# Own terms, output rows and score transposes of an RWKV-6 chunk kernel: other engines, another PSUM bank

## The chip, the cores and the metric

The kernel runs on one core of a Trainium2 chip. The metric is the device time of one execution in microseconds (us); the median of three runs of the kernel before is 248.56 us (248.35 to 248.85).

## The reference

Two blocks follow each other. The first is a recurrence over 768 positions for 4 batches x 8 heads with 48 features each; its output, written as rows of 384, is the input of a mixture-of-depths block, which picks the 128 best-scored rows of each batch, runs them through a feed-forward net and adds the gated result.

```
for t in range(S):
    cur = einsum('bhd,bhe->bhde', u * k_t, v_t)
    y[t] = einsum('bhd,bhde->bhe', r_t, state + cur)
    state = w_t * state + einsum('bhd,bhe->bhde', k_t, v_t)

scores = x @ w_gate                    # x: y as (batch, 768, 384)
top = the 128 largest of each batch
out[top] = x[top] + sigmoid(scores[top]) * (relu(x[top] @ w1) @ w2)
```

The term with `u` can be taken out of the recurrence: it adds to each row, head by head, the number sum over d of r x u x k (the *own* term), times v.

## The kernel before, in words

The sequence is cut into chunks of L = 128 positions, 6 to a batch, 24 in all (N = 24). For a chunk, the decays w are transposed (`decays_t`, L217, tile ps_w) and scanned from both sides on VectorE (`scans`, L221: right_buf, then left). r and k are transposed (`scaled`, L254, tile ps_t) and multiplied by the scans to R and K. `scores` (L274) multiplies K and R to ps_s; `masked` (L284) masks them to sc, in two VectorE instructions. `back` (L290) transposes K back and ScalarE copies it to kt. `outputs_t` (L297) multiplies sc with v and adds the product with the old state into ps_yt; ScalarE copies that to yt. `carry_products` (L350) makes the chunk's part of the state, ps_kv; `carry` (L362) adds it to the old state on VectorE (mid) and multiplies by the decays on POOL (state). A chunk that is the last of its batch has neither.

The own term: `own_products` (L260) makes r x k x u on POOL (tile rk, 128 x 8 heads x 48), `own_values` (L266) sums over the 48 to own (128 x 8) on VectorE and multiplies v by it on POOL (vo). `rows_out` (L321) transposes yt to ps_y, adds vo on VectorE into the rows x, and stores them by a DMA from the SP queue. `row_products` (L331, POOL) and `row_sums` (L335, ScalarE) make the score of each row.

The ranks need every score compared with every other. `compared_t` (L382) transposes a chunk's scores into a 128x128 tile ps_e and copies it on ScalarE to the tile every; `compared` (L397) counts on VectorE, first against the earlier chunks (L404), then against the chunk itself, read straight from ps_e (L408). After a batch's last chunk `mixture` (L413), a generator that `mix` runs a step at a time, makes ranks, picks, gathers the rows and computes the gate (with an exp on ScalarE). `forward` (L495) is the feed-forward net, cut in pieces that `fed` places between the other work of TensorE, in turns 10 and after.

The order is written by hand. `turn(i)` (L568) puts out the steps of several chunks: scores, mask, output and state of chunk i, K and R of i + 1, the decays of i + 2, the rows of i - 1, the comparisons of i - 2. Each engine works its own queue in that order. "Turn 3" in this text begins with the score products (ps_s) of chunk 3.

PSUM is split in pools with one tile buffer for each of their bufs. psW has one buffer, tag "w", used by ps_w and by ps_e. psK has one, tag "kv", used by ps_kv. psY has one, used by ps_yt and ps_y. psT has two, used by all ps_t. psS holds ps_s, psM the feed-forward net. Who takes a buffer waits until all readers of its last content are done.

Of the kernel before, what the change touches and what calls it, by code (L numbers as in the profile page):

```python
# [10 lines left out]
FP32 = mybir.dt.float32  # L11
# [3 lines left out]
AF = mybir.ActivationFunctionType  # L15
ALU = mybir.AluOpType
AX = mybir.AxisListType

L = 128
DP = 64  # L20
# [18 lines left out]
def kernel(  # L39
# [39 lines left out]
    nc = tc.nc  # L79
    PSUM = bass.MemoryType.PSUM  # L80

    B, H, S, D = r.shape
# [17 lines left out]
    psW = ctx.enter_context(tc.tile_pool(name="psW", bufs=1, space=PSUM))  # L100
# [3 lines left out]
    psK = ctx.enter_context(tc.tile_pool(name="psK", bufs=1, space=PSUM))  # L104
# [3 lines left out]
    N = len(chunks)  # L108
# [19 lines left out]
    def loads(n):  # L128

        load(v_bufs, v, n - 2)  # L130
        load(k_bufs, k, n - 1)
        load(r_bufs, r, n - 1)
        load(w_bufs, w, n)
# [22 lines left out]
    def load_weights(n):  # L156
        while n > 0 and weights:
            to, src = weights.pop(0)
            nc.sync.dma_start(out=to, in_=src)
            n -= 1  # L160
# [50 lines left out]
    def transposed(pool, tag, src):  # L211
        ps = pool.tile([L, HP, L], FP32, tag=tag, name=f"ps_{tag}")
        for j in range(HP):
            nc.tensor.transpose(ps[:, j, :], src(j), ident)  # L214
        return ps
# [48 lines left out]
        nc.gpsimd.tensor_mul(rk, rk, u_bc)  # L264

    def own_values(t):  # L266
        o = lev.tile([L, H], FP32, tag="own", name="own")
        nc.vector.tensor_reduce(out=o, in_=t.pop("rk"), axis=AX.X, op=ALU.add)  # L268
        t["vo"] = lev.tile([L, H, D], FP32, tag="vo", name="vo", bufs=3)
        nc.gpsimd.tensor_mul(  # L270
            t["vo"], v_bufs[t["n"] % VBUF][:, :, 0:D], o.to_broadcast([L, H, D])
        )
# [45 lines left out]
        t["yt"] = lev.tile([L, HP, L], FP32, tag="yt", name="yt")  # L318
        nc.scalar.copy(out=t["yt"], in_=ps)  # L319

    def rows_out(t):  # L321
        b, ci = chunks[t["n"]]
        ps = transposed(psY, "y", lambda j: t["yt"][:, j, :])
        x = t["x"] = lev.tile([L, C], FP32, tag="x", name="x", bufs=3)
        nc.vector.tensor_add(  # L325
            x.rearrange("p (h d) -> p h d", d=D),
            ps.rearrange("p j (q d) -> p (j q) d", d=DP)[:, :, 0:D], t.pop("vo"),
        )
        nc.sync.dma_start(out=views[b][b, ci * L:(ci + 1) * L, :], in_=x)

    def row_products(t):  # L331
# [10 lines left out]
    def row_scores_soon(t, x):  # L342
        b, ci = chunks[t["n"]]
        scr = lev.tile([L, C], FP32, tag="scr", name="scr")
        nc.vector.tensor_tensor_reduce(
            out=scr, in0=x, in1=wg_bc, scale=1.0, scalar=0.0, op0=ALU.mult, op1=ALU.add,
            accum_out=score[:, b, ci:ci + 1],
        )
# [33 lines left out]
    def compared_t(t):  # L382

        b, ci = chunks[t["n"]]
        if ci == 0:
            against[b] = (
                mod.tile([L, S - L], FP32, name="every", bufs=2),
                mod.tile([L, NCH, S], BF16, name="ahead", bufs=2),
                mod.tile([L, NCH, 2], FP32, name="lost", bufs=2),
            )  # L390
            nc.vector.memset(against[b][2][:, 0, 0:1], 0.0)
        t["e"] = ps = psW.tile([L, L], FP32, tag="w", name="ps_e")
        nc.tensor.transpose(ps, score[:, b, ci:ci + 1].to_broadcast([L, L]), ident)
        if ci < NCH - 1:
            nc.scalar.copy(out=against[b][0][:, ci * L:(ci + 1) * L], in_=ps)
# [137 lines left out]
    def step(f, n, *more):  # L533
        if 0 <= n < N:
            f(work.setdefault(n, dict(n=n)), *more)

    def mix(n=1):

        while n > 0 and mixing:
            try:  # L540
                next(mixing[0])
                n -= 1
            except StopIteration:
                mixing.pop(0)
# [14 lines left out]
    def fed_in_turn(n):  # L559

        if (feed or picked) and (feed or picked)[0][0] == B - 2:
            n = min(n, 1) if n < PIECES - PIECES // 2 else 0
        fed(n)
# [4 lines left out]
    def turn(i):  # L568
        step(own_products, i + 1)
        step(scores, i)  # L570
        step(masked, i)
        step(carry, i - 1, work.get(i))
        step(scaled, i + 1, "K", k_bufs, "right")
        step(back, i)
        step(rows_out, i - 1)
        if i == N:
            row_scores_soon(work[N - 1], work[N - 1]["x"])
        else:
            step(row_products, i - 1)
        step(compared_t, i - 2)  # L580
        step(compared, i - 2)
        mix()
        fed_in_turn(PIECES // 2)
        step(scaled, i + 1, "R", r_bufs, "left")
        step(decays_t, i + 2)
        step(outputs_t, i)
        step(carry_products, i)
        fed_in_turn(PIECES - PIECES // 2)
        step(scans, i + 2)
        step(range_check, i + 2)  # L590
        step(own_values, i + 1)
        if i < N:
            step(row_sums, i - 1)
        if 0 <= i - 2 < N and chunks[i - 2][1] == NCH - 1:
            mixing.append(mixture(chunks[i - 2][0]))
        mix()
        if i > -2:
            loads(i + 5)
        if i > 1:
            load_weights(1 if NCH > 2 else 100)  # L600

    with tc.manual_schedule():
        for i in range(-2, N + 1):
            turn(i)

        step(compared_t, N - 1)
        step(compared, N - 1)
        fed(NFC // 2)
        mixing.append(mixture(B - 1))
        mix(2)  # L610
        fed(NFC // 2)
        mix(2)
        fed(2 * NFC)
        mix(1000)
        fed(1000)


    def general(gen):
        u_t = gen.tile([D, H], FP32, name="u_t")
        nc.sync.dma_start(out=u_t, in_=u.rearrange("h d -> d h"))  # L620
        for b in range(B):
# [27 lines left out]
            for c in range(NCH):  # L649
                x = lev.tile([L, C], FP32, tag="x", name="x", bufs=3)  # L650
                nc.sync.dma_start(out=x, in_=out[b, c * L:(c + 1) * L, :])
                t = dict(n=b * NCH + c)
                row_scores_soon(t, x)
                compared_t(t)
                compared(t)
# [6 lines left out]
    ps = psM.tile([L, C], FP32, tag="m", name="ps_w")  # L662
# [3 lines left out]
        out=wide, in0=ps[0:1, 0:1], scalar1=0.0, scalar2=None, op0=ALU.is_gt  # L666
# [30 lines left out]
```

## Time and profile before

| | |
|---|---|
| median of 3 runs | 248.56 us |
| the profiled execution, its own time | 250.67 us |
| its span, first to last instruction | 248.9 us |
| TensorE busy | 209.1 us, 84% |
| VectorE busy | 193.7 us, 78% |
| ScalarE busy | 89.3 us, 36% |
| POOL busy | 107.3 us, 43% |

The profile is one execution, with the start and length of each instruction. PE is TensorE, PEld its weight loads, DVE VectorE, ACT ScalarE, POOL GpSimd, SP the engine that issues DMAs. A row of a timeline gives start, duration, engine, line, operation, the tile written and those read; what stands in square brackets is idle time of that engine just before, and who ended it. A row of the groups gives the count, the busy time in us, the mean of one in ns, and idle time before. A row of waits gives who waited for whom: total us, times, longest. Shares of busy time are means over the span; which wait ends last in a turn is read from its timeline.

### The profile page before, as it was taken

To read this page: it belongs to the slowest core of one execution; us is meant where nothing else is said; L and a number is where in the kernel's file an instruction comes from. 1 tells how busy PE (TensorE), PEld (TensorE's weight loads), DVE (VectorE), ACT (ScalarE), POOL (GpSimd) and SP (SyncE) were. 2 spreads that over 40 slices of the span, in tenths; PEclk is the share of its full clock that TensorE was granted. 3 is DMA by queue.
4 is the path that set the end of the run, shared out by engine and by line. 5 is a ranking of instruction groups with operands and counts; after the bars stand their busy time and mean duration, and the time that the engine had idled before them with its cause. 6 is when DMAs were issued, how large, how long until landed. Compare 5 with 4: busy or idle time off the path is not lost.

```text
span 248.9 us, 5967 instructions
## 1 busy us (share of the span) xinstructions
PE 209.1 (84%) x2290; PEld 170.4 (68%) x2290; DVE 193.7 (78%) x433; ACT 89.3 (36%) x259; POOL 107.3 (43%) x130
## 2 busy tenths in 40 slices
PE   3889889878698799888899999888899898688950
PEld 2678768766586578777578679775677687575820
DVE  6989999999999988977979989897889985513010
ACT  5423455324353254345234345424415433101100
POOL 2346664456642861564162863444344753003010
PEclk9999999999999999999999999999999999689995
DMA  8999999988986779547729765845620200001000
GB/s 127 181 179 166 193 208 231 219 204 192 176 185 135 192 108 140 117 83 121 137 40 144 156 127 101 156 97 70 128 64 15 85 32 36 32 0 34 32 18 27
DMA packets 105652, 29.17 MB, mean 117 GB/s; under 512 B 100496, under 2 KB 104848, under 8 KB 105616
## 3 DMA queue, kind: packets, MB, share of 16 engines
q1 hardware_dynamic: 105104, 27.14, 61.3%
q0 software_dynamic: 512, 1.57, 2.1%
q8 instruction: 20, 0.33, 0.6%
q14 instruction: 16, 0.13, 0.2%
HBM read 23.20 MB, written 5.51 MB: 115 GB/s over the span
## 4 chain that ended last, share of the span: by engine, by line
PE 44%; DVE 36%; issue 10%; DMA 4%; ACT 2%; POOL 1%; SPq 0%; POOLq 0%
DVE sc L288 11%; PE ps_s L279 8%; PE ps_yt L306 7%; PE ps_w L214 6%; PE ps_yt L314 6%; PE ps_h L504 5%; PE ps_f L514 5%; DVE K L258 4%; DVE x L325 4%; DVE ahead L404 4%; PE ps_kv L357 3%; DVE left L239 3%; DVE right_buf L227 2%; DVE ahead L408 2%; PE ps_t L214 2%
## 5 line engine op out<-in xcount | busy, mean ns | idle before, releaser
L270 POOL TENSOR_TENSOR vo<-v_buf,own 128x384 f32<-128x384 f32 x24 | 19.9, 831 | 85.9 <-DVE own L268 73.7
L319 ACT COPY yt<-ps_yt 128x512 f32<-128x512 f32 x24 | 14.0, 585 | 85.9 <-PE ps_yt L314 72.4
L288 DVE TENSOR_TENSOR sc<-ps_s,before_f 128x512 f32<-128x512 f32 x48 | 30.9, 685 | 12.4 <-PE ps_s L279 12.4
L214 PE MATMUL ps_w<-ident,w_buf 128*128 128x128 f32 x96 | 17.0, 303 | 20.9 <-DVE ahead L408 16.4
L239 DVE TENSOR_TENSOR_SCAN left<-ps_w,from_left 128x511 f32<-128x511 f32 x24 | 30.7, 1280 | 0.9
L227 DVE TENSOR_TENSOR_SCAN right_buf<-ps_w,from_right 128x511 f32<-128x511 f32 x24 | 29.2, 1216 | 2.5 <-PE ps_w L214 0.4
L279 PE MATMUL ps_s<-R,K 48*128 48x128 f32 x384 | 28.8, 291 | 0.3 <-DVE R L258 0.3
L504 PE MATMUL ps_h<-xeT,w 128*128 128x128 f32 x192 | 28.0, 298 | 1.3 <-ACT hid L509 0.7
L214 PEld LDWEIGHTS ps_w<-ident,w_buf 128*128 128x128 f32 x96 | 11.2, 151 | 26.0 <-DVE ahead L408 21.1
L306 PE MATMUL ps_yt<-sc,v_buf 128*64 128x128 f32 x384 | 27.1, 285 | 0.3 <-DVE x L325 0.3
L504 PEld LDWEIGHTS ps_h<-xeT,w 128*128 128x128 f32 x192 | 25.5, 209 | 2.4 <-ACT hid L509 1.0
L279 PEld LDWEIGHTS ps_s<-R,K 48*128 48x128 f32 x384 | 24.1, 193 | 3.6 <-DVE own L268 1.1
L263 POOL TENSOR_TENSOR rk<-r_buf,k_buf 128x384 f32<-128x384 f32 x24 | 24.2, 1008 | 4.7 <-DMA r_buf<-in_r_dram 4.6
L333 POOL TENSOR_TENSOR scr<-x,wg_bc 128x384 f32<-128x384 f32 x23 | 23.0, 1001 | 6.4 <-DVE x L325 4.7
L514 PE MATMUL ps_f<-w,hid 128*128 128x384 f32 x64 | 23.9, 499 | 2.1 <-ACT hid L509 2.1
L264 POOL TENSOR_TENSOR rk<-rk,u_bc 128x384 f32<-128x384 f32 x24 | 24.1, 1005 | 2.5 <-DMA u_bc<-in_u_dram 0.7
L306 PEld LDWEIGHTS ps_yt<-sc,v_buf 128*64 128x64 f32 x384 | 21.2, 140 | 4.5 <-issue 3.4
L314 PE MATMUL ps_yt<-R,state 64*48 64x128 f32 x320 | 21.5, 274 | 0.0
L293 ACT COPY kt<-ps_t 128x512 f32<-128x512 f32 x24 | 14.0, 583 | 20.5 <-PE ps_t L214 20.5
L314 PEld LDWEIGHTS ps_yt<-R,state 64*48 64x48 f32 x320 | 16.5, 119 | 3.5 <-issue 2.9
L214 PE MATMUL ps_t<-ident,r_buf 128*128 128x128 f32 x96 | 15.9, 291 | 2.1 <-ACT kt L293 0.9
L258 DVE TENSOR_TENSOR R<-ps_t,left 128x512 f32<-128x512 f32 x24 | 16.4, 683 | 0.7 <-issue 0.7
(95 smaller groups left out, 350.1 us busy)
## 6 DMA issues: line engine op xcount, KB each, us to landing
w_buf<-in_w_dram SPq DMA_DIRECT2D x24, 192.0 KB, 4.8
k_buf<-in_k_dram SPq DMA_DIRECT2D x24, 192.0 KB, 4.6
r_buf<-in_r_dram SPq DMA_DIRECT2D x24, 192.0 KB, 5.2
v_buf<-in_v_dram SPq DMA_DIRECT2D x24, 192.0 KB, 3.7
out_dram<-x SPq DMA_DIRECT2D x24, 192.0 KB, 2.0
w<-in_moe_w_dram SPq DMA_DIRECT2D x3, 512.0 KB, 5.0
w<-in_moe_w_dram SPq DMA_DIRECT2D x4, 384.0 KB, 4.3
u_bc<-in_u_dram SPq DMA_DIRECT2D x1, 192.0 KB, 4.3
```

The lines of the kernel that those rows point to most:

```text
L214: nc.tensor.transpose(ps[:, j, :], src(j), ident)
L227: nc.vector.tensor_tensor_scan(out=flat[:, W - 2::-1], data0=wt[:, W - 1:0:-1], data1=from_right.rearrange("p j t -> p (j t)")[:, W - 2::- ...
L239: nc.vector.tensor_tensor_scan(out=left.rearrange("p j t -> p (j t)")[:, 1:W], data0=wt[:, 0:W - 1], data1=start.rearrange("p j t -> p (j ...
L258: nc.vector.tensor_mul(t[name], ps, t.pop(by))
L263: nc.gpsimd.tensor_mul(rk, r_bufs[n % NBUF][:, :, 0:D], k_bufs[n % NBUF][:, :, 0:D])
L264: nc.gpsimd.tensor_mul(rk, rk, u_bc)
L279: nc.tensor.matmul(ps[:, par, j, :], t["K"][rows, j, :], t["R"][rows, j, :], start=True, stop=True,)
L288: nc.vector.tensor_mul(t["sc"][:, par], ps[:, par], _heads(before_f, HP))
L306: nc.tensor.matmul(ps[DP * par:DP * par + DP, j, :], vt[:, 2 * j + par, :], t["sc"][:, par, j, :], start=(j == 0), stop=(old is None), ski ...
L314: nc.tensor.matmul(ps[DP * par:DP * par + D, j, :], old[rows, j, :], t["R"][rows, j, :], start=False, stop=True, skip_group_check=True,)
L504: nc.tensor.matmul(ps[:, q, :], w1[:, dc, (f0 + q) * L:(f0 + q + 1) * L], xeT[:, dc, :], start=(dc == 0), stop=(dc == NDC - 1),)
L514: nc.tensor.matmul(ps, hid[:, fc, :], w2[:, fc, :], start=(fc == 0), stop=(fc == NFC - 1))
```

## The change

`own_values` sums with eight ScalarE activations (function Copy, with an accumulator output), one for each head, in place over rk, instead of one VectorE reduction. It moves from the end of turn i, where it served chunk i + 1, to the middle of turn i, ahead of `compared`, where it serves chunk i. `rows_out` copies the transposed rows from PSUM on ScalarE and adds vo on POOL; only in the last turn the VectorE addition stays. ps_e is put into psK, tag "kv", instead of psW.

```
     def own_values(t):
+        rk = t.pop("rk")
         o = lev.tile([L, H], FP32, tag="own", name="own")
-        nc.vector.tensor_reduce(out=o, in_=t.pop("rk"), axis=AX.X, op=ALU.add)
+        for h in range(H):
+            nc.scalar.activation(
+                out=rk[:, h, :], in_=rk[:, h, :], func=AF.Copy, accum_out=o[:, h:h + 1]
+            )
...
-    def rows_out(t):
+    def rows_out(t, soon=False):
         b, ci = chunks[t["n"]]
         ps = transposed(psY, "y", lambda j: t["yt"][:, j, :])
+        y = ps.rearrange("p j (q d) -> p (j q) d", d=DP)[:, :, 0:D]
         x = t["x"] = lev.tile([L, C], FP32, tag="x", name="x", bufs=3)
-        nc.vector.tensor_add(
-            x.rearrange("p (h d) -> p h d", d=D),
-            ps.rearrange("p j (q d) -> p (j q) d", d=DP)[:, :, 0:D], t.pop("vo"),
-        )
+        xh = x.rearrange("p (h d) -> p h d", d=D)
+        if soon:
+            nc.vector.tensor_add(xh, y, t.pop("vo"))
+        else:
+            nc.scalar.copy(out=xh, in_=y)
+            nc.gpsimd.tensor_add(xh, xh, t.pop("vo"))
         nc.sync.dma_start(out=views[b][b, ci * L:(ci + 1) * L, :], in_=x)
...
-        t["e"] = ps = psW.tile([L, L], FP32, tag="w", name="ps_e")
+        t["e"] = ps = psK.tile([L, L], FP32, tag="kv", name="ps_e")
         nc.tensor.transpose(ps, score[:, b, ci:ci + 1].to_broadcast([L, L]), ident)
...
-        step(rows_out, i - 1)
+        step(rows_out, i - 1, i == N)
...
         step(compared_t, i - 2)
+        step(own_values, i)
         step(compared, i - 2)
...
         step(range_check, i + 2)
-        step(own_values, i + 1)
         if i < N:
```

## Rows read from the trace of the kernel before

**Rows 1.** The page, part 1: busy us, share of the span, instructions.
```profile
PE 209.1 (84%) x2290; PEld 170.4 (68%) x2290; DVE 193.7 (78%) x433; ACT 89.3 (36%) x259; POOL 107.3 (43%) x130
```

**Rows 2.** Waits of TensorE: us in total, times, longest.
```profile
PE ps_w L214 <- DVE ahead L408: 16.4, 20, 2.1
```

**Rows 3.** Timeline of turn 3: start, us, engine, line, operation, tiles.
```profile
32.47 1.16 PE L279 MATMUL ps_s<-R,K 48*128 48x128 f32 x16
...
33.67 1.29 DVE L288 TENSOR_TENSOR sc<-ps_s,before_f 128x512 f32<-128x512 f32 x2 [0.34 <-PE ps_s L279]
...
34.69 0.58 ACT L293 COPY kt<-ps_t 128x512 f32<-128x512 f32 x1 [0.17 <-PE ps_t L214]
34.88 0.34 DVE L372 TENSOR_TENSOR mid<-ps_kv,state 128x192 f32<-128x192 f32 x1
34.92 0.27 PE L393 MATMUL ps_e<-ident,score 128*128 128x128 f32 x1
...
35.23 0.27 ACT L395 COPY every<-ps_e 128x128 f32<-128x128 f32 x1
...
35.33 0.66 PE L214 MATMUL ps_t<-ident,r_buf 128*128 128x128 f32 x4
...
36.74 0.08 DVE L408 DVE_READ_ACCUMULATOR ahead<-ps_e,score,after_f 128x1 f32 x1
...
36.88 0.66 PE L214 MATMUL ps_w<-ident,w_buf 128*128 128x128 f32 x4 [0.89 <-DVE ahead L408]
...
39.61 0.58 ACT L319 COPY yt<-ps_yt 128x512 f32<-128x512 f32 x1 [4.11 <-PE ps_yt L314]
...
40.10 1.16 PE L279 MATMUL ps_s<-R,K 48*128 48x128 f32 x16
```

**Rows 4.** Groups of instructions, whole span: count, busy us, mean ns.
```profile
L268 DVE TENSOR_REDUCE own<-rk 128x8 f32<-128x384 f32 x24 | 12.7, 527 | 0.0
L325 DVE TENSOR_TENSOR x<-ps_y,vo 128x384 f32<-128x384 f32 x24 | 13.1, 547 | 2.8 <-issue 2.8
L469 ACT COPY xeT<-ps_x 128x384 f32<-128x384 f32 x4 | 1.8, 460 | 6.7 <-PE ps_x L467 6.7
L338 ACT ACTIVATE scr<-scr 128x384 f32<-128x384 f32 x23 | 11.7, 510 | 0.0
L338 ACT ACTIVATION_READ_ACCUMULATOR scr<-scr 128x1 f32 x23 | 4.3, 187 | 0.0
L238 ACT COPY left<-from_left 128x1 f32<-128x1 f32 x24 | 4.6, 193 | 8.1 <-DVE from_left L235 8.1
L333 POOL TENSOR_TENSOR scr<-x,wg_bc 128x384 f32<-128x384 f32 x23 | 23.0, 1001 | 6.4 <-DVE x L325 4.7 <-DVE lost L391 1.5
```

**Rows 5.** Timeline of ScalarE in turn 3, operations with accumulator reads.
```profile
33.07 0.19 ACT L249 ACTIVATION_READ_ACCUMULATOR junk<-w_buf,low 128x1 f32 x1
33.30 0.61 ACT L249 ACTIVATE junk<-w_buf,high 128x384 f32<-128x384 f32 x1
...
33.82 0.19 ACT L249 ACTIVATION_READ_ACCUMULATOR junk<-w_buf,high 128x1 f32 x1
33.91 0.51 ACT L338 ACTIVATE scr<-scr 128x384 f32<-128x384 f32 x1
```

**Rows 6.** Timeline of TensorE, ps_w in turns 11 and 12.
```profile
102.27 0.66 PE L214 MATMUL ps_w<-ident,w_buf 128*128 128x128 f32 x4 [0.84 <-DVE ahead L408]
...
110.97 0.66 PE L214 MATMUL ps_w<-ident,w_buf 128*128 128x128 f32 x4 [0.71 <-DVE ahead L408]
```

**Rows 7.** Stretch: its length; busy us of PE, PEld, DVE, ACT, POOL.
```profile
62.70:72.20 9.50, 7.22 (x110) 6.05 (x108) 9.21 (x19) 3.84 (x13) 4.17 (x5) 1.00 0.98 176
```

**Rows 8.** Timeline of turn 23, TensorE and VectorE.
```profile
206.44 0.27 PE L393 MATMUL ps_e<-ident,score 128*128 128x128 f32 x1
...
206.84 0.35 DVE L372 TENSOR_TENSOR mid<-ps_kv,state 128x192 f32<-128x192 f32 x1
...
207.70 1.09 PE L306 MATMUL ps_yt<-sc,v_buf 128*64 128x128 f32 x16 [0.32 <-DVE x L325]
```

## The prediction

> **What bounds the kernel now.** I read the page first. TensorE is busy 84% of the span, VectorE 78%, ScalarE only 36% [rows 1]: two engines are nearly full, one is not. Next the waits of TensorE: one wait dwarfs the rest. The transposes of the next decays (ps_w) stood still 20 times, 16.4 us in all, for the last read of the transposed scores by VectorE (L408) [rows 2]. The reason is in the code: ps_e and ps_w share the single buffer of psW.
>
> Then the timeline of turn 3, a turn without any of the feed-forward (FFN) work [rows 3]. The reader is to see a circle. The score products start at 32.47. VectorE masks them from 33.67, adds the state (mid, ends 35.22), multiplies K, adds the rows (x), compares, and its last read ends at 36.82. Only then, at 36.88, does TensorE go on with ps_w, after 0.89 us idle, and from there it runs without a gap to the next score products at 40.10. So the turn, 7.63 us, is: TensorE 1.2, VectorE 3.15, TensorE 3.2. VectorE's own sum and the x in the middle of it set the time, because TensorE has nothing else that it may do.
>
> In turns with FFN work, 8.7 us long in turn 11, the same wait is there: 0.84 us in turn 11, 0.71 in turn 12 [rows 6]. The circle is the bound in nearly every turn. The start, and the end on the last batch's ranks, gather and FFN, are not touched.
>
> **The change, part by part.** (1) *Scores transposed into psK.* ps_w loses its wait on L408: -16.4 us if nothing replaces it [rows 2]. ps_w's remaining condition is that the scans of the turn before have read psW, which is long past. But psK holds the state products until mid has read them, so ps_e now waits for mid. Turn 3: mid ends 35.22; the hand-over from VectorE to TensorE is 0.06 (36.82 to 36.88), so ps_e starts at 35.28, not 34.92: 0.36 later. Behind it in TensorE's queue stand the FFN piece (if any), the transposes of r and ps_w. In turn 3 the r transposes began only at 35.33, held by the copy kt (34.69 + 0.58 = 35.27); now they start at 35.28 + 0.27 = 35.55, so only 0.22 is lost [rows 3]. I charge 0.22 in 7 turns without FFN work (2 to 5, 7 to 9) and 0.36 in 8 with it; turns 6, 12 and 18 follow a batch's last chunk and have no state product; in 10 and 16, where the gathered rows' transposes stand in ps_t, ps_e is late already. 7 x 0.22 + 8 x 0.36 = 4.4 us. The other end of the new edge, state products waiting for L408, is free: two groups of output products lie between.
>
> The rows of turn 3 show that the new bank is not idle when ps_e wants it, which gives 4.4 back [rows 3]. The Trainium skill (Perfetto Trace Analysis, section Matmuls) says that independent groups should rotate through different PSUM banks so that the evacuation of one overlaps the next; by that rule alone, which doesn't ask who else holds the bank, nothing would be given back (rival D).
>
> (2) *x and own leave VectorE.* Per turn 0.53 (own) and 0.55 (x) go [rows 4], 1.1 of some 7 to 8 us. Neither is subtracted again for most turns: TensorE is then the bound, and this only makes sure that VectorE keeps up. It decides around the end of a batch, where ranks and picks are added: in the stretch 62.7 to 72.2 VectorE is busy 9.21 of 9.50 us and TensorE 7.22 [rows 7]. There VectorE remains the bound at 9.21 - 1.08 = 8.1, and the gain is 1.1 to 1.4 where (1) counts 1.78 to 1.9. Charged: 0.4.
>
> (3) *x by a ScalarE copy and a POOL add.* The nearest copy, 128x384 out of PSUM, takes 460 ns (xeT); the nearest POOL operation of that shape 1001 ns [rows 4]. The copy stands between kt and the copy of the transposed scores (every): every moves from 35.2 to about 35.9, and VectorE's comparison, which follows K, waits some 0.15 us for it. psY is freed by ScalarE at about 35.7, where ps_yt needs it after 36.7. POOL's add ends about 1.5 us after kt does; its product with the gate weights, and the output DMA, start about 0.7 us later than now. On SP the loads of the turn stand behind that DMA; they are three turns ahead of their use, so I take 0 (bounds 0 to 0.7 once). POOL's sum per turn becomes some 5.4 us: no bound.
>
> (4) *own by eight ScalarE operations.* The trace has none of this shape (128x48). Bounds: 128x1 takes 193 ns, 128x384 takes 510, so 48 columns take 193 + 47 x 0.828 = 232 ns, and each is followed by an accumulator read of 187 [rows 4]. Laid end to end: 0.42 a pair, 3.35 us in all. But rows overlap: after a read the next operation starts 0.09 (33.82 to 33.91) or 0.23 later (33.07 to 33.30), and a read starts 0.10 before the end of its operation [rows 5]. With that a pair is (0.232 - 0.10) + 0.09 = 0.22, or 0.36 with the longer gap. In the 0.23 case the second operation rewrites the tile of the first; the eight write different columns, so I take the shorter: 8 x 0.23 = 1.9 us; bounds 1.8 and 3.35. ScalarE's load now is 89.3 / 24 = 3.7 us a turn at most [rows 1]; with 0.46 and 1.9 it is 6.1, below a new turn of 6.9. In turn 3: kt to 35.3, x to 35.75, every to 36.0, the eight to 37.9; the yt copy behind them, now at 39.61, is due at 38.9 [rows 3]. Covered by 1 us; with 3.35 that cover is nearly gone (39.4). vo, on POOL, ends about 38.8, and its reader is in the next turn.
>
> What is queued behind the eight: the FFN's relu (its PSUM buffer is wanted again only after the state products, covered) and, in turns 10, 16 and 22, the gate's exp, for which VectorE waits ahead of R. It can lose from nothing to one run of eight, 1.9 us, each time; VectorE arrives when about nine tenths are done, so 0.2 each, 0.5 in sum.
>
> (5) *The end.* In turn 23 TensorE has no transposes of k, r or w to do. mid ends 207.19, so ps_e goes at 207.25 instead of 206.44, and an FFN piece and ps_yt stand behind it. ps_yt had 0.32 idle (for x in psY), which goes: 0.81 - 0.32 = 0.5 us lost [rows 8]. Turn 24 keeps the old form of x.
>
> **Sum**: -16.4 + 4.4 + 0.4 + 0.5 + 0.5 = -10.6 us. Against the profiled execution's own time: 250.67 - 10.6 = 240.1. The median of the runs is 248.56, 0.9916 of that execution, so 238.1 us. The new circle: score products, mask, mid, ps_e, r, w, output and state products, 6.9 us in a plain turn, with TensorE idle for 0.2 to 0.4 in it.
>
> **Rivals.** *A: ScalarE becomes the bound in plain turns.* If a pair costs the whole 0.42 [rows 4], a plain turn of ScalarE is 3.4 now (kt, every and yt 1.4 [rows 3], the three pairs some 0.75 + 0.6 + 0.6 [rows 5]), + 0.46 + 3.35 = 7.2, 7.4 with its hand-overs, not 6.9: 0.5 lost in six or seven turns (3), 1 us each for the three exps (2.5 more than charged), 0.8 at the end, where yt's copy in turn 23 stands behind the eight. Gain 4.5: 246.2 own, 244.1 median. With 0.36 a pair: only exps and hand-overs, about 2 lost, 240. For it: pair rows of both spacings exist. Chance 0.18.
>
> *B: slower.* The trace shows no accumulating operation shorter than 128x384, and a pair spans 0.61 (33.30 to 33.91) or, with the longer gap, 0.75 [rows 5]. If that is a fixed cost and not one of the columns, the eight take 5 to 6 us, ScalarE's turn is 3.4 + 0.46 + 5.5 = 9.4, and it bounds every turn. The point from which it decides: in a plain turn of 7.63 a pair of (7.63 - 3.86) / 8 = 0.47, in an FFN turn of 8.7 one of 0.6. At 0.6 plain turns lose 1 us each (8), the exps and the end another 6, FFN turns nothing: 262 us. Against it: the 193 ns of a one-column operation. Chance 0.07. The Trainium skill (ScalarE: Activation LUTs, section Rules for kernel authors) gives adds to VectorE and not to ScalarE, which is a rule against this step; as long as ScalarE is two thirds idle the rows do not bear it out.
>
> *C: the wait only moves.* If ps_e waits for mid as long as ps_w did for L408, because VectorE falls behind through late copies of every, the gain is the shortened VectorE sum alone where it bound, 2 us or less, or nothing: 246 to 248.5. It decides when the wait for mid reaches 0.9; the rows give 0.36. Chance 0.07, half of it within 0.2%.
>
> *D: better.* ps_e finds psK free in time, since VectorE, lighter by 1.1 us a turn, comes to mid earlier: 4.4 is not given back, 235.7 own, 233.7 median; half of it gives 235.9. Against it: mid hangs on the score products of its own turn, 2.75 us after their start, whatever VectorE did before [rows 3]. Chance 0.06.
>
> **How the numbers follow.** Forecast 0.62 at 238.1 (236.8 to 240.5 with its bounds). The range takes in A and stops short of D: 236.2 to 244.3; B, C and most of D are left out, 0.2. 0.2% (0.5 us) is about what can be told from no change here. Faster: forecast, A, D and half of C, 0.89; same 0.04; slower 0.07, which is B.
>
> **What the profile after would show.** ps_w no longer waits for L408; instead ps_e waits for mid some 0.2 to 0.4 us in about 15 turns. Score products 6.9 to 7.0 us apart in turns 3 and 4. Eight ScalarE pairs a turn, 1.8 to 2 us together, and yt's copy still waiting for TensorE. VectorE's busy time down by about 26 us, ScalarE's up by 55 to 90 by its rows. I am wrong if kt or the copy yt starts late because ScalarE is behind, if a pair takes over 0.4, or if TensorE's idle before ps_e is near 0.9.

## The result and the profile after

The changed kernel takes 235.12 us (median of 4 runs, 234.40 to 237.43), against 248.7 for the kernel before on the same chip: a ratio of 0.947, 95% interval 0.941 to 0.953. The profiled execution has an own time of 237.43 (span 235.7), the longest of the four. Against the 250.67 of the profile of before that is -13.2 us; the forecast was -10.6, and its range began at 236.2. Ratios and intervals, here and below, leave out executions more than 1.5% above the fastest of their kernel; the medians do not, and the profiled executions of e2_engines, e3_bank_own and e8_own_twice are such longer ones.

Part 1 of the page of after, and the row of granted clocks from part 2 (40 slices, 9 is 90% or more):

```profile
PE 205.4 (87%) x2290; PEld 170.0 (72%) x2290; DVE 173.3 (74%) x386; ACT 141.0 (60%) x666; POOL 132.4 (56%) x153
...
PEclk9999999999999999999999999999999999799995
```

Beside [rows 1]: VectorE is 20.4 us lighter, ScalarE 51.7 us heavier, POOL 25.1. TensorE does the same work. Next the waits that follow from the changed steps (who waited for whom: total us, times, longest):

```profile
PE ps_e L400 <- DVE mid L379: 3.9, 4, 1.4
PE ps_e L400 <- ACT kt L297: 3.1, 11, 0.3
...
PE ps_e L400 <- DVE state L382: 1.0, 1, 1.0
```

The 16.4 us of ps_w [rows 2] are gone. In their place ps_e waits 8.0 us: eleven times 0.28 us (3.1 in all), and longer in turns 7 (1.03), 9 (0.46), 11 (1.35), 17 (1.36) and 23 (0.72). Where "ACT kt" is named, it is the event that came last in the records; ps_e does not read kt. In turn 3 mid ends at 34.88 and kt at 34.93, and that it is psK, still to be read by mid, for which ps_e stands is shown below by giving it another buffer.

Turn 3 of after, to lay beside [rows 3] (start, duration, engine, line, operation; in brackets the idle time before and its releaser):

```profile
32.12 1.16 PE L283 MATMUL ps_s<-R,K 48*128 48x128 f32 x16
33.33 1.29 DVE L292 TENSOR_TENSOR sc<-ps_s,before_f 128x512 f32<-128x512 f32 x2 [0.51 <-PE ps_s L283]
34.34 0.59 ACT L297 COPY kt<-ps_t 128x512 f32<-128x512 f32 x1 [0.17 <-PE ps_t L214]
34.54 0.34 DVE L379 TENSOR_TENSOR mid<-ps_kv,state 128x192 f32<-128x192 f32 x1
34.83 0.48 ACT L334 COPY x<-ps_y 128x384 f32<-128x384 f32 x1
35.03 0.29 PE L400 MATMUL ps_e<-ident,score 128*128 128x128 f32 x1 [0.28 <-ACT kt L297]
35.16 0.62 PE L214 MATMUL ps_t<-ident,r_buf 128*128 128x128 f32 x4
35.36 0.27 ACT L402 COPY every<-ps_e 128x128 f32<-128x128 f32 x1
35.49 1.00 POOL L335 TENSOR_TENSOR x<-x,vo 128x384 f32<-128x384 f32 x1
35.52 0.25 ACT L270 ACTIVATE rk<-rk 128x48 f32<-128x48 f32 x1
35.62 0.60 PE L214 MATMUL ps_w<-ident,w_buf 128*128 128x128 f32 x4
35.76 0.23 ACT L270 ACTIVATE rk<-rk 128x48 f32<-128x48 f32 x1
...
36.15 1.09 PE L310 MATMUL ps_yt<-sc,v_buf 128*64 128x128 f32 x16
37.24 0.19 ACT L270 ACTIVATION_READ_ACCUMULATOR rk<-rk 128x1 f32 x1
38.30 0.59 ACT L323 COPY yt<-ps_yt 128x512 f32<-128x512 f32 x1 [0.86 <-PE ps_yt L318]
38.78 1.16 PE L283 MATMUL ps_s<-R,K 48*128 48x128 f32 x16
```

The reader is to see four things. The turn is 6.66 us long, where it was 7.63. After ps_e nothing on TensorE waits for another engine. The eight pairs of ScalarE run from 35.52 to 37.43, 1.9 us, and the copy of yt behind them still waits 0.86 for TensorE: the cover holds. And the groups of TensorE start closer together than they last: ps_e to r 0.13, r to ps_w 0.46, ps_w to ps_yt 0.53.

Where the 13.2 us lie, by the starts of the score products in both traces (the "charged" column adds the prediction's terms up by the same stretches):

| stretch | before | after | change | charged |
|---|---|---|---|---|
| start to turn 2 | 25.09 | 25.46 | +0.37 | 0 |
| turns 2 to 9 | 63.20 | 54.73 | -8.47 | -6.67 |
| turns 10 to 21 | 108.93 | 104.46 | -4.47 | -4.55 |
| turn 22 | 7.20 | 7.64 | +0.44 | +0.17 |
| turn 23 to the span's end | 44.48 | 43.41 | -1.07 | +0.5 |
| sum | 248.9 | 235.7 | -13.2 | -10.55 |

Turns 10 to 21 agree only in the sum: turns 12, 13, 18 and 19 each gained 0.9 (0.7 charged), but turns 11 and 17 each became 0.48 longer (8.83 to 9.31, 8.83 to 9.32), where -0.48 was charged.

### The profile page after: what moved, and what is told of

It is laid out like the page before. It is cut to its first block, busy times and chain, and to the rows that moved or that the text cites. A ratio compares the mean times of both kernels' runs of the same rounds, so it can differ in the third digit from the quotient of the medians.

```text
span 235.7 us, 6339 instructions
## 1 busy us (share of the span) xinstructions
PE 205.4 (87%) x2290; PEld 170.0 (72%) x2290; DVE 173.3 (74%) x386; ACT 141.0 (60%) x666; POOL 132.4 (56%) x153
## 4 chain that ended last, share of the span: by engine, by line
PE 55%; DVE 20%; ACT 9%; issue 8%; DMA 3%; POOL 2%; POOLq 0%
PE ps_t L214 11%; PE ps_s L283 8%; PE ps_yt L310 7%; PE ps_f L521 7%; PE ps_yt L318 6%; PE ps_h L511 6%; PE ps_w L214 4%; DVE sc L292 4%; DVE left L239 3%; ACT kt L297 3%; PE ps_kv L364 3%; DVE right_buf L227 3%; DVE R L258 2%; PE ps_e L400 2%; ACT junk L249 2%
## 5 line engine op out<-in xcount | busy, mean ns | idle before, releaser
L270 ACT ACTIVATE rk<-rk 128x48 f32<-128x48 f32 x192 | 43.7, 236 | 0.0
L270 ACT ACTIVATION_READ_ACCUMULATOR rk<-rk 128x1 f32 x192 | 37.3, 194 | 0.0
L335 POOL TENSOR_TENSOR x<-x,vo 128x384 f32<-128x384 f32 x23 | 23.0, 1000 | 19.5 <-ACT x L334 19.5
L263 POOL TENSOR_TENSOR rk<-r_buf,k_buf 128x384 f32<-128x384 f32 x24 | 24.2, 1006 | 7.4 <-DMA r_buf<-in_r_dram 7.2
L511 PE MATMUL ps_h<-xeT,w 128*128 128x128 f32 x192 | 27.1, 292 | 1.3 <-ACT hid L516 0.7
L283 PEld LDWEIGHTS ps_s<-R,K 48*128 48x128 f32 x384 | 24.3, 194 | 4.0 <-issue 1.6
L340 POOL TENSOR_TENSOR scr<-x,wg_bc 128x384 f32<-128x384 f32 x23 | 25.5, 1108 | 1.8
L511 PEld LDWEIGHTS ps_h<-xeT,w 128*128 128x128 f32 x192 | 24.7, 204 | 2.3 <-ACT hid L516 0.9
L380 POOL TENSOR_TENSOR state<-mid,all 128x192 f32<-128x192 f32 x16 | 8.1, 506 | 27.8 <-DVE mid L379 27.8
L214 PE MATMUL ps_w<-ident,w_buf 128*128 128x128 f32 x96 | 15.8, 291 | 4.8 <-DMA w_buf<-in_w_dram 4.2
```

Of the source, the lines that this page charges most:

```text
L263: nc.gpsimd.tensor_mul(rk, r_bufs[n % NBUF][:, :, 0:D], k_bufs[n % NBUF][:, :, 0:D])
L270: nc.scalar.activation(out=rk[:, h, :], in_=rk[:, h, :], func=AF.Copy, accum_out=o[:, h:h + 1])
L283: nc.tensor.matmul(ps[:, par, j, :], t["K"][rows, j, :], t["R"][rows, j, :], start=True, stop=True,)
L340: nc.gpsimd.tensor_mul(t["scr"], t.pop("x"), wg_bc)
L511: nc.tensor.matmul(ps[:, q, :], w1[:, dc, (f0 + q) * L:(f0 + q + 1) * L], xeT[:, dc, :], start=(dc == 0), stop=(dc == NDC - 1),)
```

## The experiments

Three questions: which part brings the gain; what the wait of ps_e costs, and whether ScalarE's load matters; what happened in turns 11 and 17. Whole executions of one kernel scatter by 1 to 2%, and the traces differ in parts that the edits hardly touch: by 2.4 us up to turn 2 (23.16 in e9, 25.58 in e1) and by 4.0 behind the start of turn 23 (41.0 to 45.0). So the table takes stretches of the traces beside the ratios: T2 to T7, T7 to T10 and T10 to T23 mean from the score products of chunk 2 to those of chunk 7, and so on. ps_e's bank and the engines of own and x are in the second column.

| run | what it is | median us | ratio [95%] | T2-T7 | T7-T10 | T10-T23 | sum |
|---|---|---|---|---|---|---|---|
| before | psW; VectorE, VectorE | 248.7 | | 36.85 | 26.35 | 116.13 | 179.33 |
| after | psK; ScalarE, ScalarE + POOL | 235.12 | 0.947 [0.941, 0.953] | 31.72 | 23.01 | 112.10 | 166.83 |
| e1_bank | psK; VectorE, VectorE | 240.71 | 0.963 [0.954, 0.972] | 33.13 | 27.53 | 110.58 | 171.24 |
| e2_engines | psW; ScalarE, ScalarE + POOL | 239.07 | 0.954 [0.945, 0.963] | 34.51 | 23.68 | 113.37 | 171.56 |
| e3_bank_own | psK; ScalarE, VectorE | 237.64 | 0.941 [0.930, 0.952] | 31.90 | 25.86 | 110.56 | 168.32 |
| e4_bank_x | psK; VectorE, ScalarE + POOL | 239.41 | 0.959 [0.951, 0.968] | 31.72 | 26.65 | 111.76 | 170.13 |
| e5_in_psS | after, ps_e in psS | 234.10 | 0.941 [0.932, 0.950] | 31.14 | 23.06 | 110.40 | 164.60 |
| e6_behind_r | after, ps_e behind r | 232.36 | 0.932 [0.923, 0.940] | 32.17 | 22.47 | 108.86 | 163.50 |
| e7_no_clash | after, POOL free at the gate | 235.59 | 0.942 [0.931, 0.952] | 31.72 | 23.03 | 111.28 | 166.03 |
| e8_own_twice | after, own summed twice | 250.46 | 1.004 [0.999, 1.008] | 33.86 | 24.32 | 120.71 | 178.89 |
| e9_behind_r_psS | e5 and e6 together | 228.84 | 0.922 [0.916, 0.929] | 31.73 | 22.91 | 106.01 | 160.65 |
| e10_x_by_turn | e9, x on VectorE from turn 10 | 229.04 | 0.921 [0.914, 0.928] | 31.76 | 22.90 | 106.71 | 161.37 |
| e11_own_psS | e3, ps_e in psS | 233.88 (one run) | | 31.67 | 24.61 | 108.83 | 165.11 |

### The bank alone, and the engines alone

e1 is the kernel before with one line changed:

```diff
-        t["e"] = ps = psW.tile([L, L], FP32, tag="w", name="ps_e")
+        t["e"] = ps = psK.tile([L, L], FP32, tag="kv", name="ps_e")
```

> The kernel before with one edit: the transposed scores go to psK; own and the rows x stay on VectorE. By the prediction's sum the bank alone is worth 16.4 - 4.4 = 12 us, so 237. Theory V (VectorE takes over): once ps_w no longer waits, a plain turn is VectorE's own sum, 7.15 us in turn 3 (7.63 less its two waits of 0.34 and 0.14), not 6.66; the turns at the end of batch 0, where VectorE was full already, gain nothing; the FFN turns gain what they gain in the full change. That is 2 + 0.3 + 4.5 us, so 242.

e2 is the changed kernel with that line undone:

```diff
-        t["e"] = ps = psK.tile([L, L], FP32, tag="kv", name="ps_e")
+        t["e"] = ps = psW.tile([L, L], FP32, tag="w", name="ps_e")
```

> The full change but with the transposed scores left in psW: own on ScalarE, x on ScalarE and POOL. Theory V: the circle stays (ps_w behind L408), shortened by the 0.46 us that x took in it, less some 0.15 for the later copy of the scores; 20 turns of 0.3, and 1.5 more where VectorE was full: 248.6 - 7.5 = 241. Rival: own and x only lighten an engine that isn't the bound, so without the bank nothing is gained: 247 to 248.5.

e1 was expected at 242 and took 240.71; e2 was expected at 241 and took 239.07, so its rival (nothing gained without the bank) is out. From turn 2 to turn 23 the bank alone brings 8.1 us, where the prediction's sum has 12 for it (1.6 of the difference is the lower clock of turn 7, below); the engines alone bring 7.8, both together 12.5. So each covers a part of the other: a turn was one circle through both engines, and it becomes shorter either by taking work out of VectorE's half or by letting TensorE go on during it. With the bank alone the plain turns are 6.66, 6.71, 6.96 and 6.48 long: the first two have the length of after's, not theory V's 7.15; then VectorE falls behind, and ps_e waits 0.58 and 0.71 for mid in turns 4 and 5, where it waits 0.28 in after. In turns 10 to 22 the bank alone (110.58) is better than the whole change (112.10).

### Own alone and x alone, with the bank

e3 leaves x on VectorE:

```diff
-        step(rows_out, i - 1, i == N)
+        step(rows_out, i - 1, True)
```

> The full change but with x added by VectorE straight from PSUM in all turns (no ScalarE copy of x, no POOL addition). Theory V: VectorE's plain turn becomes 6.7 us, about TensorE's 6.66; 0.45 us a turn come back in the four turns around the end of batch 0, but POOL is lighter by 1 us a turn and the gate's small operations on VectorE stand less behind POOL: 235 to 237. Rival (every engine move counts): 240, half way to the bank alone.

e4 takes own back to VectorE, at its old place in the turn:

```diff
-        for h in range(H):
-            nc.scalar.activation(
-                out=rk[:, h, :], in_=rk[:, h, :], func=AF.Copy, accum_out=o[:, h:h + 1]
-            )
+        nc.vector.tensor_reduce(out=o, in_=rk, axis=AX.X, op=ALU.add)
...
-        step(own_values, i)
...
+        step(own_values, i + 1)
```

> The full change but with own summed by VectorE at its old place (end of the turn, for the next chunk). Theory V: VectorE's plain turn 6.7 to 6.85 us: 0.1 to 0.2 lost in plain turns, 0.45 in the four turns around the end of batch 0, exp of the gate no longer behind the eight: 237. Rival: the eight ScalarE pairs cost more than they spare, and this one is faster than the full change: 234 or less.

Either one alone brings the turns 2 to 6 to within 0.2 us of after's (31.90, 31.72, 31.72): there 0.5 us off VectorE is enough and the second 0.5 is worth nothing. Both are wanted only in turns 7 and 9, around the first batch's ranks and picks (turn 9: 8.10 in after, 8.64 and 9.21 in e3 and e4, 9.80 in e1). And in turns 10 to 22 moving x costs something: e4 is 1.2 longer than e1, after 1.5 longer than e3, while moving own changes nothing (e1 and e3 differ by 0.02). For the whole time, e3's interval [0.930, 0.952] holds after's ratio: x on ScalarE and POOL is worth nothing that can be told. e3 was expected at 235 to 237, and the two executions that its ratio rests on took 234.01 and 235.89; e4 was expected at 237 and took 239.41.

In the profiled executions of e3 and e4 turn 7 shows a second loss. TensorE's rows from e4's turn 7, then its windows before and after the end of the wait (stretch, length, busy time and count of PE, PEld, DVE, ACT, POOL, granted clock, DMA share, GB/s):

```profile
61.27 0.29 PE L397 MATMUL ps_e<-ident,score 128*128 128x128 f32 x1 [1.94 <-DVE state L379]
...
62.39 1.96 PE L307 MATMUL ps_yt<-sc,v_buf 128*64 128x128 f32 x16
64.28 1.83 PE L315 MATMUL ps_yt<-R,state 64*48 64x128 f32 x16
```

```profile
56.71:61.30 4.59, 2.65 (x33) 2.32 (x29) 4.49 (x9) 3.11 (x10) 2.81 (x4) 1.00 1.28 233
61.30:67.25 5.95, 5.95 (x78) 5.11 (x78) 5.81 (x13) 1.09 (x3) 3.67 (x5) 0.71 1.13 216
```

and the same two windows of after:

```profile
57.18:60.80 3.62, 2.62 (x32) 2.26 (x29) 3.52 (x8) 3.08 (x11) 2.74 (x3) 1.00 1.04 257
60.80:65.19 4.39, 4.36 (x79) 3.79 (x79) 4.21 (x10) 2.96 (x20) 4.11 (x5) 1.00 1.15 198
```

ps_e waits 1.94 (VectorE is busy 4.49 of 4.59), and then the output products run at the lower of the two clocks, 1.2 GHz: 1.96 instead of 1.09 us. The second window does the same work in 5.95 instead of 4.39. In e1 the wait was 2.23 and the window 5.98 at 0.71. In e3 they are 1.77, and 6.02 at 0.72. In after the wait is 1.03 and the clock stays at 2.4 GHz.

This loss does not belong to e3 as a kernel. Its four executions took 239.39 (the profiled one) and 239.72 us at a mean granted clock of 0.970 and 0.969, and 234.01 and 235.89 at 0.992 and 0.990. The lower clock at the very end, which every trace here has, takes 0.007 to 0.010 of the mean, and the one in turn 7 another 0.007; an execution at 0.992 or 0.990 has no room for both. So the two shorter executions ran turn 7 at the higher clock. Without the 1.6 us by which that window is longer than after's (6.02 against 4.39) e3's stretch T7 to T10 would be some 24.3, an estimate: x on ScalarE and POOL saves about 1.3 us there and costs 1.5 in turns 10 to 22, which fits the ratios. Whether the other executions of e1 and e4 had the loss is not shown.

### Another bank, another order

e5 puts ps_e into psS, where nothing but the score products lives; e6 leaves it in psK and puts the transposes of r ahead of it; e9 does both:

```diff
-        t["e"] = ps = psK.tile([L, L], FP32, tag="kv", name="ps_e")
+        t["e"] = ps = psS.tile([L, L], FP32, tag="s", name="ps_e")
```

```diff
-        step(compared_t, i - 2)
-        step(own_values, i)
-        step(compared, i - 2)
         ... (gathered rows, feed-forward piece, transposes of r)
+        step(compared_t, i - 2)
+        step(own_values, i)
+        step(compared, i - 2)
```

> The changed kernel with the transposed scores in psS (the bank of the score products), so that ps_e waits for the mask only and not for mid. Theory M (the wait of ps_e for mid is TensorE's last idle time in most turns): the 0.28 us go in FFN turns; in plain turns the r transposes stand behind kt, so 0.15 to 0.2 there: 7 x 0.18 + 8 x 0.28, and the long waits of 1.0 to 1.4 shrink by 0.25 each: 4 us less, 231. Rival: the copy kt, or VectorE's sum, takes the wait's place: less than 1 us, 234 to 235.

> The changed kernel with the order changed: transposing the scores, own's sums and the comparisons stand behind the FFN piece and the transposes of r, not ahead of them. Theory M: by then mid is long done, so no wait of ps_e is left in FFN turns (0.28 to 1.36 each); in plain turns the r transposes wait for kt instead, some 0.3: 3 to 5 us less, 230 to 232. Rival: the comparisons come too late for VectorE, whose scans then start later: 235 or more.

> The order of the run before last (score transposes, own's sums and comparisons behind the transposes of r) together with psS as the bank of the transposed scores, so that neither ps_e waits for mid nor the state products for the last read of ps_e. Theory M (what is left of TensorE's idle time in the turns is these waits): the 3.0 us that the state products waited for L415 go, the 3.6 us of the r transposes behind kt stay: 2.5 us less than that run, 230. Rival: the score products of the next turn now wait for L415, which comes late in the turns with the gate; nothing is gained, 232.

In psS the 0.28 us waits are gone, plain turns are 6.52 instead of 6.66, and the stretch from turn 2 to turn 23 is 2.2 shorter, where 4 was expected; this is the price of psK still being read by mid. The long waits shrink only to 0.91, 1.09 and 1.10 in turns 7, 11 and 17, and by the medians alone (234.10, intervals overlapping) e5 can't be told from after. The order is worth 3.3: turns 11 and 17 go from 9.3 to 7.8, while turns 10 and 16 grow from 8.8 to 9.5 and 9.6; the median, 232.36, is just above the expected 230 to 232. But it leaves a wait on the far side of the edge, for the last read of ps_e:

```profile
PE ps_t L214 <- ACT kt L297: 3.6, 9, 0.9
PE ps_kv L364 <- DVE ahead L415: 3.0, 6, 1.1
```

These are e6's waits; in e9 the second is gone. e9, at 228.84 (expected 230), is with e10, from which it can't be told apart, the best version found: 0.922 of before, its interval below that of after.

### The doubled own sum

```diff
-        for h in range(H):
-            nc.scalar.activation(
-                out=rk[:, h, :], in_=rk[:, h, :], func=AF.Copy, accum_out=o[:, h:h + 1]
-            )
+        o2 = lev.tile([L, H], FP32, tag="own2", name="own2")
+        for to in (o2, o):
+            for h in range(H):
+                nc.scalar.activation(
+                    out=rk[:, h, :], in_=rk[:, h, :], func=AF.Copy, accum_out=to[:, h:h + 1]
+                )
```

> The changed kernel with the eight sums done twice (16 ScalarE pairs a turn; the first eight go to a tile that nobody reads). Doubles the disputed cost, from 1.8 to 3.6 us a turn. By the cover that was reckoned (1 us in a plain turn), ScalarE is then the bound: 3.4 + 0.46 + 3.6 = 7.5 to 7.7 us a plain turn instead of 6.66, 8 turns; the gate's exp comes 1.8 later in turns 10, 16 and 22, and yt's copy in turn 23 up to 1: 235 + 7 + 4 = 244 to 246. Rival: ScalarE runs ahead and hides it all: 235 to 236.

In turn 3 the sixteen pairs begin at 35.81 and are 0.225 apart, as the eight are. Plain turns are 6.87, 7.03 and 7.04, not 7.5 to 7.7: of 1.8 us more on ScalarE only 0.2 to 0.4 reaches a plain turn. In turns 10, 11, 16, 17 and 22 it comes through more fully (10.36, 10.67, 10.14, 10.66, 9.38; 1.3 to 1.7 above after). VectorE waits 4.7 us in all, up to 1.5 each, for the gate's exp behind the pairs, where it waits 1.1 in after. From turn 2 to turn 23 that makes 12.1 us, and the median, 250.46, lies above the expected 244 to 246: the plain turns lost less than reckoned, the turns at and behind the gate more. So rival A's mechanism exists, at about twice the real price: the 1.9 us of the change lie in cover that 3.7 us would use up.

### Turns 11 and 17, and the clash with POOL

Turn 10 and 11 of after:

```profile
84.31 1.01 DVE L482 CUSTOM_DVE_ANT_0 scr<-xe,wg_bc 128x384 f32<-128x384 f32 x1
84.98 1.20 POOL L340 TENSOR_TENSOR scr<-x,wg_bc 128x384 f32<-128x384 f32 x1
85.36 0.83 DVE L487 SCALAR_TENSOR_TENSOR neg<-own 128x1 f32<-128x1 f32 x1
...
86.92 1.00 POOL L263 TENSOR_TENSOR rk<-r_buf,k_buf 128x384 f32<-128x384 f32 x1
87.02 0.93 DVE L498 TENSOR_TENSOR gate<-gate,den 128x1 f32<-128x1 f32 x1
87.86 0.68 DVE L258 TENSOR_TENSOR R<-ps_t,left 128x512 f32<-128x512 f32 x1
...
92.49 0.35 DVE L379 TENSOR_TENSOR mid<-ps_kv,state 128x192 f32<-128x192 f32 x1
92.99 0.29 PE L400 MATMUL ps_e<-ident,score 128*128 128x128 f32 x1 [1.35 <-DVE mid L379]
```

and the same two VectorE instructions in the kernel before:

```profile
93.71 0.16 DVE L480 SCALAR_TENSOR_TENSOR neg<-own 128x1 f32<-128x1 f32 x1
...
94.59 0.16 DVE L491 TENSOR_TENSOR gate<-gate,den 128x1 f32<-128x1 f32 x1
```

Two instructions of one column take 0.83 and 0.93 instead of 0.16. Each ends where the POOL instruction that it overlaps ends, to 0.03 us: 85.36 + 0.83 = 86.19, and 84.98 + 1.20 = 86.18; 87.02 + 0.93 = 87.95, and 86.92 + 1.00 = 87.92. POOL's products now lie where VectorE is at the gate. R is late behind it, the next mask is, and in turn 11 ps_e waits 1.35 for mid. The Trainium skill ("SBUF — State Buffer", section "Who interferes with whom") states that a VectorE instruction with two inputs in SBUF contends with a GpSimd instruction that reads SBUF, and that the order of issue decides who blocks; these rows agree, and they give the size.

e7 takes away POOL's product over 384 columns (it does one) in the three turns:

```diff
-        nc.gpsimd.tensor_mul(t["scr"], t.pop("x"), wg_bc)
+        if t["n"] in (9, 15, 21):
+            nc.gpsimd.tensor_mul(t["scr"][:, 0:1], t.pop("x")[:, 0:1], wg_bc[:, 0:1])
+        else:
+            nc.gpsimd.tensor_mul(t["scr"], t.pop("x"), wg_bc)
...
+        if t["n"] in (9, 15, 21):
+            scr = scr[:, 0:1]
```

> The changed kernel, but the products of the rows with the gate weights are made for one of 384 columns only for chunks 9, 15 and 21 (their scores are then not the reference's), so that POOL is not at work when the gate's operations on one column run on VectorE in turns 10, 16 and 22. Theory P (VectorE's operations with two SBUF inputs stand still while POOL's runs): neg (L487) falls from 0.83 to 0.16 us, R comes 0.7 earlier in these turns, the wait of ps_e for mid in turns 11 and 17 falls from 1.35 to about 0.7, and turn 22 is 0.7 shorter: 2 us less, 233. Rival: neg is slow because of ScalarE's run of eight or by itself: it stays at 0.83, and so does the time.

```profile
84.57 0.16 DVE L492 SCALAR_TENSOR_TENSOR neg<-own 128x1 f32<-128x1 f32 x1
...
85.86 1.00 POOL L263 TENSOR_TENSOR rk<-r_buf,k_buf 128x384 f32<-128x384 f32 x1
85.95 0.93 DVE L503 TENSOR_TENSOR gate<-gate,den 128x1 f32<-128x1 f32 x1
```

In e7 neg is back at 0.16, and turns 11, 17 and 22 are 0.27 shorter each, 0.8 together. The expected 2 us did not come, because gate falls behind POOL's next instruction (L263) as it did in after. The clash is shown for neg, with its price.

Which move brings which clash can be read from e4 (x moved, own on VectorE) and e3 (own moved, x on VectorE), turn 10, e4 first:

```profile
88.54 0.83 DVE L484 SCALAR_TENSOR_TENSOR neg<-own 128x1 f32<-128x1 f32 x1
...
90.08 0.16 DVE L495 TENSOR_TENSOR gate<-gate,den 128x1 f32<-128x1 f32 x1
```

```profile
88.23 0.16 DVE L487 SCALAR_TENSOR_TENSOR neg<-own 128x1 f32<-128x1 f32 x1
...
89.13 0.93 DVE L498 TENSOR_TENSOR gate<-gate,den 128x1 f32<-128x1 f32 x1
```

In turn 10 moving x makes neg late and moving own makes gate late; turn 16 gives the same numbers. gate's clash alone leaves turns 10 to 22 of e3 as long as those of e1 (110.56 and 110.58), where gate takes 0.16 in all three turns; what it costs beside neg's was not isolated.

e10 tries the other way round, on e9: x by VectorE in the turns from 10 on, by `step(rows_out, i - 1, i == N or i >= 10)`.

> As the run beside it, with x added by VectorE from turn 10 on (where the FFN makes TensorE's turn long and VectorE has room) and by ScalarE and POOL only in turns up to 9. Theory P (in the FFN turns the POOL addition costs more, by keeping VectorE's two-input operations of the gate waiting, than it spares VectorE): 1 to 2 us less than the run beside it, 228 to 229; neg in turn 10 takes 0.16 us, not 0.83. Rival: VectorE's 0.55 us a turn count in these turns too: 1 to 3 us more.

T10 to T23 is 106.71 against e9's 106.01: no gain (229.04 against 228.84), and neg is still 0.83 there (0.86 in e9), since POOL's product with the gate weights still lies beside it. So the 1.2 to 1.5 us that x costs in the order of after is not a fixed price of the move: in the order of e9 keeping x on VectorE gains nothing. That what POOL happens to do beside the gate decides this fits the rows, but is not shown for the whole 1.2 to 1.5.

### Is it the wait that brings the lower clock in turn 7?

e11 is e3 with ps_e in psS (the line of e5).

> The run with own on ScalarE and x on VectorE, but with the transposed scores in psS instead of psK. In that run turn 7 took 10.3 us: TensorE had stood still 1.8 us ahead of ps_e, and the granted clock of the rest of the turn was near half. Theory K (the long stop ahead of ps_e lets the clock fall): ps_e waits for the mask and not for the state's product, 0.3 to 0.6 us less; if that suffices, turn 7 is 8.0 to 8.5 us at a granted clock of 1.00, and the stretch from turn 2 to turn 23 is 3 to 4 us shorter than in that run, 164 to 165. Rival: the clock falls at that place for another reason: turn 7 stays at 10 us or more.

TensorE's windows of turn 7, before and after its wait:

```profile
57.19:61.20 4.01, 2.62 (x32) 2.26 (x28) 3.90 (x7) 2.83 (x11) 2.68 (x3) 1.00 0.99 239
61.20:65.71 4.51, 4.43 (x78) 3.80 (x79) 4.41 (x12) 2.40 (x18) 3.14 (x4) 1.00 1.03 206
```

The wait ahead of ps_e is 1.42 (1.77 in e3), the clock stays at 2.4 GHz, and the turn is 8.52 instead of 10.32. That fits a clock that falls after a long wait: 1.77, 1.94 and 2.23 with a fall (e3, e4, e1), 1.03 and 1.42 without. But the kernel before waited 2.14 in the same turn, ahead of ps_w, and kept 2.4 GHz (its row, then its windows before and after it):

```profile
67.61 0.66 PE L214 MATMUL ps_w<-ident,w_buf 128*128 128x128 f32 x4 [2.14 <-DVE ahead L408]
...
61.94:67.61 5.67, 3.39 (x38) 2.82 (x34) 5.60 (x14) 2.73 (x9) 3.49 (x4) 1.00 1.00 174
67.61:71.44 3.83, 3.83 (x74) 3.23 (x74) 3.58 (x6) 1.10 (x4) 0.26 (x1) 1.00 1.00 185
```

So the length of one wait does not settle it. Nor does e11, a single execution: two of e3's own four executions ran turn 7 without the fall, by their mean clocks (above), with ps_e still in psK. What makes the clock fall in turn 7 stays open.

## Why the prediction was right in kind and too small

**Right.** The circle was the bound in the plain turns, and its last wait went as described. A pair costs 0.225 us (0.23 taken; 236 and 194 ns by the groups, start to start less), eight of them 1.9; the copy of x takes 0.48 (0.46). ScalarE has cover left (0.86 ahead of yt's copy, 1 us reckoned): +51.7 us busy, just under the 55 to 90 given. ps_e waits in place of ps_w; where nothing else is late it is 0.28 (0.22 and 0.36 charged). Turn 23 lost 0.52 up to the rows of the last chunk (6.82 to 7.34), 0.5 charged; its ps_e waits 0.72 for mid. Rival B did not occur; A's price was not reached, and e8 shows where it would begin. D did not occur either, though the time came out near it: psK is not free in time, and e5 prices that at 2.2 us.

**Too small, term (1) and the new circle.** In turns 2 to 9 the change brought 8.47 us where 6.67 was charged. The 1.8 more is 0.30 in each of turns 2 to 5 and 8, 0.22 in turn 6 and 0.14 in turn 9; turn 7, with its 0.4 charged for VectorE, came out as reckoned (1.49 for 1.52). The step that failed is reckoning TensorE's queue by the durations of its rows, where distances between starts were wanted. It stands in the new circle of 6.9, which lays the groups end to end behind ps_e (0.27, then 0.66 for r), and in the term of -16.4, whose idle times begin where the row before ends. In the trace of after the starts follow each other by 0.13 and 0.46: the rows overlap. ps_e begins 2.91 after the score products (2.81 by the prediction's steps), yet ps_w begins at 3.50, not 3.74, and the turn is 6.66. In turn 3 of before [rows 3] r's row ends at 35.99, and the 0.89 of ps_w's wait is counted from there; with the 0.46 of after ps_w would have started at 35.79, so 1.09 was to be had. That is 0.20 of the 0.30; 0.04 is r, which lost 0.18 instead of 0.22, and 0.06 lies behind ps_w, from which the next score products are 3.16 away instead of 3.22. [rows 3] could not show the distance, since r waits for kt there and ps_w for L408; the trace of before has it elsewhere, as in turn 7, where the transposes of k, K and yt and ps_e begin at 63.03, 63.52, 63.96 and 64.40, with rows of 0.66 and 0.60.

**Too small, the end.** +0.5 was charged for the last stretch, and between the two profiled executions it came out at -1.07. The 0.52 in turn 23 is there; the other 1.6 lie behind it, where the edits change little (ps_e's bank). The row of clocks bears on it: the 35th slice of after has 7, the 35th and 36th of before 6 and 8:

```profile
PEclk9999999999999999999999999999999999689995
```

By windows, from the rows of the last chunk on, of before and then of after:

```profile
211.24:215.00 3.76, 2.37 (x14) 2.03 (x13) 3.46 (x13) 0.27 (x1) 0.00 (x0) 0.74 0.14 52
215.00:218.00 3.00, 2.31 (x11) 2.17 (x11) 0.00 (x0) 0.60 (x1) 0.00 (x0) 0.50 0.00 0
```

```profile
199.63:203.40 3.77, 1.76 (x14) 1.38 (x13) 3.47 (x13) 0.85 (x2) 0.00 (x0) 1.00 0.14 52
203.40:206.40 3.00, 2.94 (x14) 2.94 (x15) 0.00 (x0) 0.01 (x1) 0.00 (x0) 0.52 0.00 0
```

Before runs the same 14 matmuls at a mean of 0.74 and goes to the lower clock (0.50) behind them; after keeps the higher one for the first and falls (0.52) in the second. The products of the last ranks stand behind the feed-forward products that run in these windows, of before and then of after:

```profile
219.83 0.68 PE L419 MATMUL ps_r<-ones,ahead 128*128 128x1 bf16 x21
```

```profile
207.20 0.67 PE L426 MATMUL ps_r<-ones,ahead 128*128 128x1 bf16 x21
```

From the rows of the last chunk they are 8.59 and 7.57 away: 1.0 of the 1.6. In all traces this distance follows the clock: from the last addition to rank before them (`rank<-rank,behind_n`) to these products it is 4.7 to 5.2 us in the three whose granted clock here was 0.57 to 0.58, 4.0 to 4.2 at 0.79 and 2.5 at 1.00 (last section). From there to VectorE's last instruction both take the same (21.0). The other 0.6 lies behind that instruction (8.06 and 7.46 to the end of the span), and its cause stays open.

**What is left of the miss.** Turns 2 to 22 give -12.50 and turn 23 +0.52, together -12.0 where -10.55 was charged. Taken from the median of 248.56 that would be 236.6, an estimate, inside the range; the measured 235.12 is 1.5 lower. That part is not in these stretches. It lies in the start and the end, where executions differ, or in the scatter of the medians: the interval of the ratio reaches from 234.1 to 236.9.

**Wrong, terms (2) and (3).** Term (3) put the addition on POOL at 0, by its load alone (5.4 us a turn), and missed that POOL's instructions move in time against VectorE's; own's move, term (2), does the same at gate. VectorE's busy time fell by 20.4 where some 26 was forecast; neg in three turns (0.67 each) and gate in two (0.77) are 3.5 us of the difference. Turns 11 and 17 became longer instead of shorter, with ps_e waiting 1.35 for mid where 0.36 was charged. Term (1) is also not worth its 12 us by itself: e1 shows 8.1, or 9.7 without the lower clock of its turn 7, and the rest of the 12.5 comes only with own and x off VectorE. That turns 10 to 21 hit their sum, -4.47 for -4.55, is a cancellation. The 0.5 for the exps, (4), was not lost either: VectorE waits 0.27 for each exp, as it did before (1.1 in four, in both traces); it loses by the clash.

**What the prediction did not see at all**: that in turn 7 a longer wait can be followed by the lower clock, 1.6 us for the same work. In the profiled executions of e1, e3 and e4 it was; all other traces ran that turn at the higher clock. It is in the 23.01 of after against 25.86 and 26.65 (e3 and e4) from T7 to T10, but since two executions of e3 had no such loss, it is no sure gain of the full change.

## What to carry to other kernels

When a tile is moved to another buffer, ask who else holds that buffer at that time, and look for one that nobody holds: psS was worth 2.2 us over psK from turn 2 to turn 23, and the order 3.3. Sum up a queue of matmul groups by the distance of their starts, not by their durations. When work goes to POOL, look at which VectorE instructions with two SBUF operands its instructions will lie beside: here 0.67 us for neg in three turns, while POOL was busy for only 56% of the span.

## What the runs showed of the hardware that was not expected

- A VectorE instruction of one column, two operands in SBUF, that meets a running POOL instruction of 128x384 lasts until that one ends: 0.83 and 0.93 us instead of 0.16. POOL's took 1.20 instead of 1.00 when it began while a VectorE instruction (L482) was under way.
- In turn 3 of after the group behind four transposes of 128x128 starts 0.43 to 0.53 us after them, though their row gives 0.60 to 0.66; one alone is followed after 0.13, though its row gives 0.29.
- The granted clock of the sparse end differs from execution to execution: over the same 8 us (from 8 to 16 us after the last score products) 0.57 to 0.58 in before, e3 and e8, 0.79 in after, e2, e6, e7 and e9, 1.00 in the others. The end lasts 44.2 to 45.0, 42.0 to 43.4 and 41.0 to 42.3 us. Each is one execution of another kernel. That one kernel does both is seen in the mean clocks of after: 237.43 and 235.15 us at 0.982, 234.40 and 235.08 at 0.991. These times overlap, so the clock is not the whole of the scatter.
- 1.8 us more on an engine that is 60% busy cost 0.2 to 0.4 in a plain turn and 1.3 to 1.7 in the turns where another engine waits for what is queued behind it, and in those after them (e8).
